# Decode attention with a gated feed-forward: K turned by VectorE in 32x32 blocks instead of by TensorE through PSUM

## The chip, the cores and the metric

One core of one Trainium2 chip. The time is device microseconds of one execution of the whole program; the kernel before takes 231.77 us, the median of three runs (231.77 to 231.87). Engines are named as the profile names them: PE (TensorE), PEld (its weight loads), DVE (VectorE), ACT (ScalarE), POOL (GpSimd), and SP, whose queue issues nearly all DMA transfers.

## The reference, cut to what matters

```
xn = layernorm(x)                                   # x: [2, 1, 512], two sequences, one new token each
q  = (xn @ wq) as 32 heads of 128                   # 8 K/V heads, 4 query heads to each
k, v = the last 4096 positions of k_cache, v_cache  # [2, 8, 4096, 128] of [2, 8, 32768, 128]
p  = softmax(q . k / sqrt(128)) over the 4096 positions
A  = (p . v as [2, 4096]) @ wo
B  = ((gate * (gate > 0)) * up) @ W_down            # gate = xn @ W_gate, up = xn @ W_up, 1792 wide
out = x + A + B                                     # [2, 1, 512], all float32
```

## The kernel before

All data are float32. Everything large is read once: wq, W_gate and W_up, then K and V, then W_down and wo, 94.9 MB together.

**Loads.** `load` (L69) takes a tile from the pool `ring`, which has four slots (`RING = 4`, L17), and issues one transfer on SP's queue (L71). A load waits until the tile that had its slot four loads earlier has been read for the last time; later loads wait behind it on the same queue. The order of the loads through the ring is wq in two halves, W_gate, W_up, then for groups 0 to 3 the K tiles, with the V tiles of the group before in between: k0_0, k0_1, k1_0, v0_0, k1_1, v0_1, k2_0, v1_0, k2_1, v1_1, k3_0, v2_0, k3_1, v2_1, v3_0, v3_1, then W_down and wo in two halves (wo0, wo1; wo1 in five pieces).

**Groups.** A group g is one sequence and four K/V heads (`C = 4`), so there are `NG = 4` groups. A K or V tile (g, a), with a = 0 or 1, holds two heads h: partitions are 64 blocks of 64 consecutive positions for each of the two heads interleaved with them (row p = 2y + h), and each row has 64 positions times 128 values (4.19 MB).

**From K to scores.** `transposes` (L248) turns K on PE: 64 products with the identity for each tile, 128x128 each (L256), four to a PSUM bank, and each bank is copied to the tile kT in SBUF (L245), by ACT and DVE in turn. `scores` (L262) multiplies kT with the query columns qz (L269): 16 products a tile, over the 128 values of a head, 512 positions each, four of them at a time in the four quarters of PE's columns. `kwork` (L375) delays scores by half a tile and places the steps of the last group's `softmax` (L275) between the transposes, step by step, so that PE, DVE and ACT work on different banks at the same time.

**Softmax and values.** `softmax` finds the maximum (L278, L281, L283, L287, L293, L297), takes the exponential on ACT with its row sums (L302), turns the probabilities on PE (L313) and copies them out with a mask (L314). `values` (L326) multiplies them with the V tile (L333, 16 products) and DVE masks the result into `on` (L339). `gather` (L346) sums over rows on PE (L350), `finish` (L355) adds up and scales (L360, L361), and `spread_heads` (L363) puts two finished groups into the layout of the last projection (L366).

**Order.** The pool is under a manual schedule: each engine runs its instructions in the order of the program text (the loops from L391 on), and waits where an operand or a buffer is not ready. For each group g from 1 to 3 and each a: load k(g, a), load v(g-1, a), K work of (g, a) with softmax of g-1 inside it where a = 0, then values of (g-1, a). After the loops come the last softmax, the last values, the products with W_down and wo (L430, L434) and the output.

Of the kernel before, what the change touches and what calls it, by code (L numbers as in the profile page):

```python
# [20 lines left out]
def kernel(  # L21
# [89 lines left out]
    NSLOT = C * S1  # L111
    qz = const.tile([P, NG, NSLOT * 36], F32, name="qz")
    nc.gpsimd.memset(qz, 0.0)
    ones = const.tile([1, 1], F32, name="ones")
# [7 lines left out]
    spread = const.tile([HR, NE, HR, NE], F32, name="spread")  # L122
    nc.gpsimd.memset(spread, 0.0)
    for e in range(NE):
        nc.gpsimd.tensor_copy(spread[:, e, :, e], ident[0:HR, 0:HR])
# [18 lines left out]
    by_h = const.tile([P, NP, HK], F32, name="by_h")  # L144
    nc.vector.tensor_reduce(
        out=by_h, in_=ident.rearrange("p (q a s k) -> p a k q s", q=Q, a=NP, s=S1), op=ALU.add, axis=AX.XY
    )

    half_of = const.tile([P, 2], F32, name="half_of")
    nc.vector.tensor_reduce(  # L150
        out=half_of, in_=ident.rearrange("p (y h) -> p h y", h=2), op=ALU.add, axis=AX.X
    )
    own = const.tile([P, 2, REP], F32, name="own")
    nc.vector.tensor_copy(own, half_of[:, :, None].to_broadcast([P, 2, REP]))

# [18 lines left out]
    xn = const.tile([B, D], F32, name="xn")  # L174
# [29 lines left out]
    for r in range(R):  # L204
        qs = work.tile([P, 512], F32, name=f"qs{r}", tag="qs")
        (nc.vector.tensor_copy if r else nc.scalar.copy)(qs, q_ps[r])
        qt = ps_kt.tile([P, REP, C, 16, B], F32, name=f"qt{r}", tag="kt")
        for i in range(REP):
            nc.tensor.transpose(  # L209
                qt[:, i].rearrange("p c s b -> p (c s b)"), qs[:, i * P:(i + 1) * P], ident  # L210
            )
        for b in range(B):
            dst = qz[:, r * B + b].rearrange("p (a s h k) -> p a s h k", a=NP, s=S1, h=2)
            for h in range(2):
                nc.vector.tensor_copy(  # L215
                    dst[:, :, :, h, 0:REP], qt[:, :, h::2, 0:S1, b].rearrange("p i a s -> p a s i")
                )

# [12 lines left out]
    gr = work.tile([P, FQ], F32, name="gr", tag="gr", bufs=1)  # L231
# [7 lines left out]
    HW = W // S1  # L239
    ss, pts, rls = {}, {}, {}  # L240
    kts, osb = {}, {}
    turn = [0]

    def evacuate(dst, src):
        (nc.vector.tensor_copy if turn[0] % 2 else nc.scalar.copy)(dst, src)  # L245
        turn[0] += 1

    def transposes(g, a, s1, kt_in):  # L248

        kt = ktp.tile([P, 2, HW], F32, name=f"kT{g}_{a}_{s1}", tag="kT")  # L250
        kts[g, a, s1] = kt
        for n in range(2 * Q):
            pk = ps_kt.tile([P, 512], F32, name=f"pk{g}_{a}_{s1}_{n}", tag="kt")
            for u in range(4):
                j = 8 * Q * s1 + 4 * n + u
                nc.tensor.transpose(pk[:, u * P:(u + 1) * P], kt_in[:, j * P:(j + 1) * P], ident)  # L256
            evacuate(
                kt[:, :, n * 256:(n + 1) * 256], pk.rearrange("p (y h) -> p h y", h=2),
            )
            yield  # L260

    def scores(g, a, s1):  # L262
        if (a, s1) == (0, 0):
            ss[g] = ps_s.tile([P, 512], F32, name=f"s{g}", tag="s")
        kt = kts.pop((g, a, s1))
        for h in range(2):
            n = (a * S1 + s1) * 2 + h
            for q in range(Q):
                nc.tensor.matmul(  # L269
                    ss[g][32 * q:32 * q + 32, :], qz[:, g, 32 * n:32 * n + 32],  # L270
                    kt[:, h, q * 512:(q + 1) * 512],
                    start=(a == 0 and s1 == 0 and h == 0), stop=(a == NP - 1 and s1 == S1 - 1 and h == 1),
                )

    def softmax(g):  # L275

        m = work.tile([P, 1], F32, name=f"m{g}", tag="m")
        nc.vector.tensor_reduce(out=m, in_=ss[g], op=ALU.max, axis=AX.X)  # L278
        yield
        mt = ps_1.tile([1, P], F32, name=f"mt{g}", tag="misc")  # L280
        nc.tensor.transpose(mt, m, ident)  # L281
        mx = work.tile([1, NP, HK], F32, name=f"mx{g}", tag="mx")
        nc.vector.tensor_reduce(  # L283
            out=mx, in_=mt.rearrange("p (q a s k) -> p a k q s", q=Q, a=NP, s=S1), op=ALU.max, axis=AX.XY
        )
        mb = work.tile([1, NP, S1, HK], F32, name=f"mb{g}", tag="mb")
        nc.vector.tensor_scalar(  # L287
            mb, mx[:, :, None, :].to_broadcast([1, NP, S1, HK]), -SCALE, None, op0=ALU.mult
        )
        yield  # L290
        nm_ps = ps_1.tile([P, 1], F32, name=f"nm_ps{g}", tag="misc")
        for q in range(Q):
            nc.tensor.matmul(  # L293
                nm_ps[32 * q:32 * q + 32, :], mb.rearrange("p a s k -> p (a s k)"), ones, start=True, stop=True
            )
        nm = work.tile([P, 1], F32, name=f"nm{g}", tag="nm")
        nc.vector.tensor_copy(nm, nm_ps)  # L297

        p = work.tile([P, 512, 2], F32, name=f"p{g}", tag="p", bufs=1)
        l = work.tile([P, 1], F32, name=f"l{g}", tag="l")  # L300
        both = ss[g][:, :, None].to_broadcast([P, 512, 2])
        nc.scalar.activation(p, both, AF.Exp, bias=nm, scale=SCALE, accum_out=l)  # L302
        yield
        yield
        yield

        pts[g] = work.tile([P, 2, Q * NP * S1, 4, HK], F32, name=f"pt{g}", tag="pt")
        pv = p.rearrange("r y h -> r (y h)")
        for jh in range(2):
            pp = ps_kt.tile([P, 4, P], F32, name=f"pp{g}_{jh}", tag="kt")  # L310
            for u in range(4):
                lo = (4 * jh + u) * P
                nc.tensor.transpose(pp[:, u], pv[:, lo:lo + P], ident)  # L313
            nc.vector.tensor_tensor(  # L314
                pts[g][:, jh].rearrange("p n u k -> p u n k"), pp.rearrange("p u (n k) -> p u n k", k=HK),
                own.rearrange("p h i -> p (h i)")[:, None, None, :].to_broadcast([P, 4, Q * NP * S1, HK]), op=ALU.mult,
            )
            yield
        lp = ps_1.tile([HR, 1], F32, name=f"lp{g}", tag="misc")
        nc.tensor.matmul(lp, by_h.rearrange("p a k -> p (a k)"), l, start=True, stop=True)  # L320
        rls[g] = work.tile([HR, 1], F32, name=f"rl{g}", tag="rl")
        nc.vector.reciprocal(rls[g], lp)
# [3 lines left out]
    def values(g, a, v):  # L326
        o = ps_1.tile([P, 512], F32, name=f"o{g}_{a}", tag=f"o{a}")
        for s1 in range(S1):
            for jh in range(2):
                for q in range(Q):  # L330
                    n = (q * NP + a) * S1 + s1
                    lo = (8 * Q * s1 + 8 * q + 4 * jh) * P
                    nc.tensor.matmul(  # L333
                        o[32 * q:32 * q + 32, :],
                        pts[g][:, jh, n].rearrange("p u k -> p (u k)"), v[:, lo:lo + 512],
                        start=(s1 == 0 and jh == 0), stop=(s1 == S1 - 1 and jh == 1),
                    )
# [17 lines left out]
    def finish(g):  # L355
        r, b = divmod(g, B)
        if b == 0:
            osb[r] = const.tile([HR, B, P], F32, name=f"osb{r}")
        od = work.tile([HR, P], F32, name=f"od{g}", tag="od")
        nc.vector.tensor_reduce(out=od, in_=oa[g].rearrange("h u d -> h d u"), op=ALU.add, axis=AX.X)  # L360
        nc.vector.tensor_scalar(osb[r][:, b], od, rls[g], 2.0, op0=ALU.mult, op1=ALU.mult)  # L361

    def spread_heads(r):  # L363
        op = ps_1.tile([P, NJ, B], F32, name=f"op{r}", tag="misc")
        for e in range(NE):
            nc.tensor.matmul(  # L366
                op, spread[:, e].rearrange("h k e -> h (k e)"),
# [5 lines left out]
    pend = []  # L373

    def kwork(g, a, kt_in, others=()):  # L375

        others = list(others)
        for s1 in range(S1):
            for n, _ in enumerate(transposes(g, a, s1, kt_in)):
                if n > 1 and others and next(others[0], "end") == "end":  # L380
                    others.pop(0)
                if (a, s1, n) == (0, 0, 1) and pend:
                    scores(*pend.pop())
            if pend:
                scores(*pend.pop())
            pend.append((g, a, s1))
        for o in others:
            for _ in o:
                pass

    for a in range(NP):  # L391
        kwork(0, a, load_kv(k_cache, "k", 0, a))
    for g in range(1, NG):
        for a in range(NP):
            kt_in = load_kv(k_cache, "k", g, a)
            v_in = load_kv(v_cache, "v", g - 1, a)
            kwork(g, a, kt_in, [softmax(g - 1)] if a == 0 else [])
            if a:
                gather(g - 1, a - 1)
# [6 lines left out]
    scores(*pend.pop())  # L406
    vin = [load_kv(v_cache, "v", g, a) for a in range(NP)]
    dw = load_down()
    for _ in softmax(g):
        pass  # L410
# [43 lines left out]
    yw = work.tile([P, D], F32, name="yw", tag="yw", bufs=1)  # L454
# [38 lines left out]
```

## Time and profile before

| | before |
|---|---|
| time, median of 3 runs (us) | 231.77 |
| profiled execution: time / span of its instructions (us) | 231.71 / 229.9 |
| busy, share of the span: PE / PEld / DVE / ACT | 79% / 42% / 32% / 20% |
| bytes read from HBM, mean rate over the span | 94.90 MB, 413 GB/s |
| mean granted PE clock, share of full speed | 0.925 |

How to read it: the span runs from the first to the last instruction of the profiled execution; its time contains it and 1.8 us around it. A busy share is an average over stages. In lists of groups a row gives line, engine, operation, output<-inputs, shapes and count, then busy time in all and the mean duration of one in ns, then the idle time ahead of them and who ended it. In the chain of waits and in timelines a row begins with start and duration in us. In the view by windows a row has the stretch, then for PE, PEld, DVE, ACT and POOL the busy time and count, then granted PE clock, busy share of the DMA engines, and GB/s. On PE a float32 product shows as two records.

### The profile page before, as it was taken

Reading aid. Unit: us, or ns where it says so; the run is one execution under the profiler, and the core shown is the slowest. Engines: PE = TensorE matmul, PEld = TensorE weight load, DVE = VectorE, ACT = ScalarE, POOL = GpSimd, SP = SyncE. Lnnn points to the kernel's source line nnn. Section 1 sums busy time; section 2 is a strip of 40 time slices with the busy share of each in tenths; the row PEclk is TensorE's granted clock in tenths of the full one; section 3 lists DMA queues with packets and bytes.
Section 4 is the critical chain, followed back from the end, with each engine's and each line's share of the span. In section 5 each row is a group of like instructions: output and inputs, shape, how many; then the busy total and the mean of one; then the engine's idle time right before and its main releaser. Section 6 shows DMA issues by size and latency. Waiting matters only on the chain.

```text
span 229.9 us, 3250 instructions
## 1 busy us (share of the span) xinstructions
PE 182.2 (79%) x1432; PEld 96.0 (42%) x1432; DVE 73.3 (32%) x143; ACT 46.6 (20%) x78; POOL 3.8 (2%) x17
## 2 busy tenths in 40 slices
PE   0483970819999889998899699589999965889493
PEld 0430230219666573661583563248566213124011
DVE  2400021024444561641572441247244144111000
ACT  2000100004444550440351340025134002000001
POOL 6000000000000000000000000000000000000000
PEclk9998598576999999999999999889999996799799
DMA  7999999999999999999999999999999999999980
GB/s 274 456 433 391 464 409 466 399 445 450 422 408 450 436 410 423 448 428 413 439 450 419 416 446 442 410 422 456 425 410 436 445 422 430 428 445 405 420 339 14
DMA packets 3921, 95.10 MB, mean 414 GB/s; under 512 B 442, under 2 KB 450, under 8 KB 836
## 3 DMA queue, kind: packets, MB, share of 16 engines
q1 hardware_dynamic: 3896, 94.90, 96.4%
q8 instruction: 11, 0.18, 0.3%
q14 instruction: 2, 0.02, 0.0%
q10 hardware_dynamic: 12, 0.01, 0.0%
HBM read 94.90 MB, written 0.00 MB: 413 GB/s over the span
## 4 chain that ended last, share of the span: by engine, by line
PE 51%; DMA 41%; DVE 4%; ACT 2%; issue 1%; SPq 1%
DMA k<-in_A_k_cache_dram 25%; PE pk L256 23%; PE s L269 11%; DMA wo<-in_A_wo_dram 10%; PE o L333 9%; DMA wq<-in_A_wq_dram 5%; PE q_ps L198 3%; PE pp L313 2%; ACT p L302 2%; PE oa L350 2%; DVE kT L245 1%; PE op L366 1%; SPq L449 1%; DVE on L339 1%; PE nm_ps L293 0%
## 5 line engine op out<-in xcount | busy, mean ns | idle before, releaser
L256 PE MATMUL pk<-ident,k 128*128 128x128 f32 x512 | 67.3, 286 | 8.4 <-DMA k<-in_A_k_cache_dram 8.4
L256 PEld LDWEIGHTS pk<-ident,k 128*128 128x128 f32 x512 | 57.7, 146 | 24.6 <-issue 21.0
L245 ACT COPY kT<-pk 128x512 f32<-128x512 f32 x64 | 37.5, 586 | 100.1 <-PE pk L256 100.1
L245 DVE COPY kT<-pk 128x512 f32<-128x512 f32 x64 | 44.2, 691 | 37.9 <-PE pk L256 37.8
L333 PE MATMUL o<-v,pt 128*32 128x512 f32 x256 | 34.2, 627 | 0.0
L269 PE MATMUL s<-kT,qz 128*32 128x512 f32 x256 | 32.1, 607 | 0.0
L339 DVE TENSOR_TENSOR on<-o,own_u 128x512 f32<-128x512 f32 x8 | 5.5, 692 | 39.4 <-PE o L333 39.4
L333 PEld LDWEIGHTS o<-v,pt 128*32 128x32 f32 x256 | 8.9, 114 | 20.0 <-issue 19.9
L198 PE MATMUL q_ps<-wq,xnT 128*32 128x512 f32 x64 | 12.3, 940 | 4.3 <-DMA wq<-in_A_wq_dram 4.3
L269 PEld LDWEIGHTS s<-kT,qz 128*32 128x32 f32 x256 | 7.0, 111 | 13.2 <-issue 13.2
L350 PE MATMUL oa<-on,pick 128*16 128x512 f32 x16 | 8.2, 596 | 4.2 <-DVE on L339 4.2
L430 PE MATMUL yw_ps<-wo,oT 128*2 128x512 f32 x56 | 7.9, 703 | 3.9 <-DMA wo<-in_A_wo_dram 3.9
L186 PE MATMUL xt_ps<-rep,xn 2*128 2x32 f32 x16 | 3.7, 402 | 8.7 <-DVE rep L179 8.7
L225 PE MATMUL u_ps<-wu,xnT 128*32 128x448 f32 x32 | 5.2, 816 | 6.6 <-DMA wu<-in_B_W_up_dram 6.6
L198 PEld LDWEIGHTS q_ps<-wq,xnT 128*32 128x32 f32 x64 | 2.9, 163 | 12.9 <-issue 7.6
L313 PE MATMUL pp<-ident,p 128*128 128x128 f32 x32 | 5.5, 306 | 2.4 <-ACT p L302 1.5
L455 ACT COPY yw<-yw_ps 128x512 f32<-128x512 f32 x1 | 0.6, 586 | 33.3 <-PE yw_ps L430 33.3
L186 PEld LDWEIGHTS xt_ps<-rep,xn 2*128 2x128 f32 x16 | 3.6, 319 | 8.7 <-DVE rep L179 8.7
L302 ACT ACTIVATE p<-s,nm 128x1024 f32<-128x1024 f32 x4 | 4.5, 1115 | 13.0 <-DVE nm L297 12.9
L314 DVE TENSOR_TENSOR pt<-pp,own 128x512 f32<-128x512 f32 x8 | 5.5, 692 | 3.8 <-PE pp L313 3.7
L215 DVE COPY qz<-qt 128x16 f32<-128x16 f32 x8 | 0.8, 167 | 17.6 <-PE qt L209 17.6
L225 PEld LDWEIGHTS u_ps<-wu,xnT 128*32 128x32 f32 x32 | 1.3, 160 | 10.5 <-DMA wu<-in_B_W_up_dram 7.4
(72 smaller groups left out, 60.9 us busy)
## 6 DMA issues: line engine op xcount, KB each, us to landing
k<-in_A_k_cache_dram SPq DMA_DIRECT2D x8, 4096.0 KB, 29.1
v<-in_A_v_cache_dram SPq DMA_DIRECT2D x8, 4096.0 KB, 29.0
wq<-in_A_wq_dram SPq DMA_DIRECT2D x2, 4096.0 KB, 16.9
wo<-in_A_wo_dram SPq DMA_DIRECT2D x1, 4096.0 KB, 31.7
wg<-in_B_W_gate_dram SPq DMA_DIRECT2D x1, 3584.0 KB, 29.6
wu<-in_B_W_up_dram SPq DMA_DIRECT2D x1, 3584.0 KB
wd<-in_B_W_down_dram SPq DMA_DIRECT2D x1, 3584.0 KB
wo<-in_A_wo_dram SPq DMA_DIRECT2D x1, 2048.0 KB, 20.7
```

Source lines behind the costliest of these rows:

```text
L186: nc.tensor.matmul(xt_ps[:, v, kc, :], lhsT, rep16.rearrange("r s b -> r (s b)"), start=True, stop=True)
L198: nc.tensor.matmul(q_ps[r][32 * c:32 * c + 32, :], xnT[:, 0, kc, :], wqt[kc // 2][:, kc % 2, n * 512:(n + 1) * 512], start=(kc == 0), stop ...
L225: nc.tensor.matmul(dst[32 * c:32 * c + 32, :], xnT[:, 1, kc, :], wt[:, kc, c * FQ:(c + 1) * FQ], start=(kc == 0), stop=(kc == KC - 1),)
L245: (nc.vector.tensor_copy if turn[0] % 2 else nc.scalar.copy)(dst, src)
L256: nc.tensor.transpose(pk[:, u * P:(u + 1) * P], kt_in[:, j * P:(j + 1) * P], ident)
L269: nc.tensor.matmul(ss[g][32 * q:32 * q + 32, :], qz[:, g, 32 * n:32 * n + 32], kt[:, h, q * 512:(q + 1) * 512], start=(a == 0 and s1 == 0 ...
L302: nc.scalar.activation(p, both, AF.Exp, bias=nm, scale=SCALE, accum_out=l)
L313: nc.tensor.transpose(pp[:, u], pv[:, lo:lo + P], ident)
L333: nc.tensor.matmul(o[32 * q:32 * q + 32, :], pts[g][:, jh, n].rearrange("p u k -> p (u k)"), v[:, lo:lo + 512], start=(s1 == 0 and jh == 0 ...
L339: nc.vector.tensor_tensor(ons[a], o.rearrange("p (u d) -> p u d", u=4), own_u[:, :, None].to_broadcast([P, 4, P]), op=ALU.mult)
L350: nc.tensor.matmul(oa[g].rearrange("h u d -> h (u d)"), pick[:, 8 - 8 * a:24 - 8 * a], ons[a].rearrange("p u d -> p (u d)"), start=(a == 0 ...
L430: nc.tensor.matmul(yw_ps[32 * c:32 * c + B, :], lhsT, w, start=(n < Q), stop=(n >= wide - Q))
```

## The change

K is no longer turned by PE. For each half tile DVE turns 32x32 blocks of [128, 4096] values with four `transpose` instructions of 128x1024, from SBUF to SBUF (new function `keys`). After that, a lane quarter (32 partitions) of kT holds 32 of the 128 values of a head, for the 32 rows of K that lay in that quarter. A score product therefore runs over 32 values (index m) for four sets of positions at once: its weights qz hold the query in block-diagonal form, one block for each lane quarter x, and m = 0 to 3 accumulates in PSUM. There are still 16 products of 512 columns for each tile; their moving operand takes every second element (`h::2`), because the two heads alternate in the turned rows.

The 16 products read the turned tile whole, and the pool for kT has room for one tile (two halves), as before.

The probabilities go into pz, every second element for each head, in two exponentials of 64 partitions; DVE turns pz in 32x32 blocks, and 16 copies of 32 partitions, by ACT and DVE in turn, move the blocks to the lane quarters where V needs them. The softmax of group g now stands in the program text right after the scores of (g, 1), as one piece, ahead of gather and values of group g-1; the step-by-step interleaving is gone. The setup of qz is done by 32 small copies on ACT and DVE, some constants are smaller or share memory, and a factor 2 is taken elsewhere.

```diff
+    JS = J // S1
+    NB = DH // 32
+    qz = const.tile([P, NG, NB, NP, 2, 32], F32, name="qz")
     nc.gpsimd.memset(qz, 0.0)
+    pz = const.tile([P, JS, 32], F32, name="pz")
+    nc.gpsimd.memset(pz, 0.0)
...
+        for m in range(NB):
+            src = qt[32 * m:32 * m + 32, :, :, 0].rearrange("p i (t h) b -> p b t h i", h=2)
+            for x in range(Q):
+                d = qz[32 * x:32 * x + 32, r * B:r * B + B, m]
+                dst = bass.AP(
+                    tensor=d.tensor, offset=d.offset + x * TK,
+                    ap=[d.ap[0], d.ap[1], [64 + REP, NP], [32, 2], [1, REP]],
                 )
+                (nc.vector.tensor_copy if x % 2 else nc.scalar.copy)(dst, src)
...
-    def transposes(g, a, s1, kt_in):
...
-    def scores(g, a, s1):
...
+    CUT = 4
+
+    def keys(g, a, kt_in):
+
+        if a == 0:
             ss[g] = ps_s.tile([P, 512], F32, name=f"s{g}", tag="s")
+        kts = []
+        for s1 in range(S1):
+            kt = ktp.tile([P, JS, NB, 32], F32, name=f"kT{g}_{a}_{s1}", tag="kT")
+            n = JS // CUT
+            for c in range(CUT):
+                lo = (s1 * JS + c * n) * DH
+                nc.vector.transpose(
+                    kt[:, c * n:(c + 1) * n].rearrange("p j m k -> p (j m k)"), kt_in[:, lo:lo + n * DH]
                 )
+            kts.append(kt)
+        for m in range(NB):
+            for h in range(2):
+                for s1 in range(S1):
+                    q = 2 * h + s1
+                    nc.tensor.matmul(
+                        ss[g][32 * q:32 * q + 32, :], qz[:, g, m, a, h], kts[s1][:, :, m, h::2],
+                        start=(a == 0 and m == 0), stop=(a == NP - 1 and m == NB - 1),
+                    )
...
+        pv = pz.rearrange("p j (i h) -> p j i h", h=2)
+        for h in range(2):
+            o = slice(PK * h, PK * h + PK)
+            nc.scalar.activation(
+                pv[o, :, :, h], ss[g][o].rearrange("p (j i) -> p j i", j=JS), AF.Exp, bias=nm[o], scale=SCALE, accum_out=l[o],
             )
+        pT = work.tile([P, JS, Q, NP, REP], F32, name=f"pT{g}", tag="pT", bufs=1)
+        nc.vector.transpose(pT.rearrange("p j x t k -> p (j x t k)"), pz.rearrange("p j s -> p (j s)"))
+        pts[g] = work.tile([P, NP, S1, JS, 2, REP], F32, name=f"pt{g}", tag="pt")
+        n = 0
+        for h in range(2):
+            for s1 in range(S1):
+                q = 32 * (2 * h + s1)
+                for x in range(Q):
+                    (nc.vector.tensor_copy if n % 2 else nc.scalar.copy)(
+                        pts[g][32 * x:32 * x + 32, :, s1, :, h], pT[q:q + 32, :, x].rearrange("p j t k -> p t j k")
+                    )
+                    n += 1
...
     for a in range(NP):
-        kwork(0, a, load_kv(k_cache, "k", 0, a))
+        keys(0, a, load_kv(k_cache, "k", 0, a))
+    softmax(0)
     for g in range(1, NG):
         for a in range(NP):
             kt_in = load_kv(k_cache, "k", g, a)
             v_in = load_kv(v_cache, "v", g - 1, a)
-            kwork(g, a, kt_in, [softmax(g - 1)] if a == 0 else [])
+            keys(g, a, kt_in)
             if a:
+                softmax(g)
                 gather(g - 1, a - 1)
             elif g % B == 1 and g > 1:
                 spread_heads((g - 2) // B)
...
     g = NG - 1
-    scores(*pend.pop())
     vin = [load_kv(v_cache, "v", g, a) for a in range(NP)]
     dw = load_down()
-    for _ in softmax(g):
-        pass
```

More of the change, by code (lines that the diff above doesn't have):

```diff
@@ L109 @@
     make_identity(nc, ident)
-    NSLOT = C * S1
-    qz = const.tile([P, NG, NSLOT * 36], F32, name="qz")
+    JS = J // S1
+    NB = DH // 32
+    qz = const.tile([P, NG, NB, NP, 2, 32], F32, name="qz")
     nc.gpsimd.memset(qz, 0.0)
+    pz = const.tile([P, JS, 32], F32, name="pz")
+    nc.gpsimd.memset(pz, 0.0)
     ones = const.tile([1, 1], F32, name="ones")
@@ L120 @@
     oT = const.tile([P, R, NJ, B], F32, name="oT")
-    spread = const.tile([HR, NE, HR, NE], F32, name="spread")
+    spread = const.tile([HR, HR + 1, NE], F32, name="spread")
     nc.gpsimd.memset(spread, 0.0)
-    for e in range(NE):
-        nc.gpsimd.tensor_copy(spread[:, e, :, e], ident[0:HR, 0:HR])
+    nc.gpsimd.tensor_copy(spread[:, 0:HR, NE - 1], ident[0:HR, 0:HR])
     pick = const.tile([P, 24], F32, name="pick")
@@ L143 @@
     HK = 2 * REP
[L144 to L154, printed above, removed]
+    TK = NP * REP
+    by_h = const.tile([P, NP, 2, REP], F32, name="by_h")
+    for h in range(2):
+        nc.vector.tensor_reduce(
+            out=by_h[:, :, h], in_=ident[:, PK * h:PK * h + PK].rearrange("p (x t k) -> p t k x", t=NP, k=REP),
+            op=ALU.add, axis=AX.X,
+        )
     stats = const.tile([B, 6], F32, name="stats")
@@ L173 @@
     nc.vector.tensor_scalar(xc, x2, mv[:, 0:1], 2.0, op0=ALU.subtract, op1=ALU.mult)
-    xn = const.tile([B, D], F32, name="xn")
+    xn = xc
     nc.vector.tensor_scalar(xn, xc, rs2, None, op0=ALU.mult)
@@ L211 @@
             )
[L212 to L216, printed above, removed]
+        for m in range(NB):
[5 more added lines that the diff above has]
+                    ap=[d.ap[0], d.ap[1], [64 + REP, NP], [32, 2], [1, REP]],
                 )
+                (nc.vector.tensor_copy if x % 2 else nc.scalar.copy)(dst, src)
     g_ps = ps_kt.tile([P, FQ], F32, name="g_ps", tag="kt")
@@ L230 @@
     nc.scalar.copy(gs, g_ps)
-    gr = work.tile([P, FQ], F32, name="gr", tag="gr", bufs=1)
+    gr = gs
     nc.vector.scalar_tensor_tensor(gr, gs, 0.0, gs, op0=ALU.is_gt, op1=ALU.mult)
@@ L235 @@
     nc.vector.transpose(hT, hh.rearrange("p (w k) -> p k w", k=FB))
-    HW = W // S1
     ss, pts, rls = {}, {}, {}
[L241 to L246, printed above, removed]
-    def transposes(g, a, s1, kt_in):
[L250 to L260, printed above, removed]
-    def scores(g, a, s1):
-        if (a, s1) == (0, 0):
-            ss[g] = ps_s.tile([P, 512], F32, name=f"s{g}", tag="s")
[L265 to L272, printed above, removed]
-                )
+    osb = {}
+    CUT = 4
+    def keys(g, a, kt_in):
+        if a == 0:
+            ss[g] = ps_s.tile([P, 512], F32, name=f"s{g}", tag="s")
+        kts = []
[6 more added lines that the diff above has]
+                    kt[:, c * n:(c + 1) * n].rearrange("p j m k -> p (j m k)"), kt_in[:, lo:lo + n * DH]
+                )
+            kts.append(kt)
[7 more added lines that the diff above has]
+                    )
     def softmax(g):
@@ L278, in softmax @@
         nc.vector.tensor_reduce(out=m, in_=ss[g], op=ALU.max, axis=AX.X)
-        yield
         mt = ps_1.tile([1, P], F32, name=f"mt{g}", tag="misc")
         nc.tensor.transpose(mt, m, ident)
-        mx = work.tile([1, NP, HK], F32, name=f"mx{g}", tag="mx")
+        mx = work.tile([1, 2, TK], F32, name=f"mx{g}", tag="mx")
         nc.vector.tensor_reduce(
-            out=mx, in_=mt.rearrange("p (q a s k) -> p a k q s", q=Q, a=NP, s=S1), op=ALU.max, axis=AX.XY
+            out=mx, in_=mt.rearrange("p (h x k) -> p h k x", h=2, k=TK), op=ALU.max, axis=AX.X
@@ L285, in softmax @@
         )
-        mb = work.tile([1, NP, S1, HK], F32, name=f"mb{g}", tag="mb")
+        mb = work.tile([1, 2, S1 * Q, TK], F32, name=f"mb{g}", tag="mb")
         nc.vector.tensor_scalar(
-            mb, mx[:, :, None, :].to_broadcast([1, NP, S1, HK]), -SCALE, None, op0=ALU.mult
+            mb, mx[:, :, None, :].to_broadcast([1, 2, S1 * Q, TK]), -SCALE, None, op0=ALU.mult
         )
-        yield
         nm_ps = ps_1.tile([P, 1], F32, name=f"nm_ps{g}", tag="misc")
[L292 to L295, printed above, removed]
+        nc.tensor.matmul(nm_ps, mb.rearrange("p h x k -> p (h x k)"), ones, start=True, stop=True)
@@ L296, in softmax @@
         nm = work.tile([P, 1], F32, name=f"nm{g}", tag="nm")
         nc.vector.tensor_copy(nm, nm_ps)
-        p = work.tile([P, 512, 2], F32, name=f"p{g}", tag="p", bufs=1)
         l = work.tile([P, 1], F32, name=f"l{g}", tag="l")
[L301 to L316, printed above, removed]
-            )
-            yield
+        pv = pz.rearrange("p j (i h) -> p j i h", h=2)
@@ L319, in softmax @@
+        n = 0
+        for h in range(2):
+            for s1 in range(S1):
[3 more added lines that the diff above has]
+                        pts[g][32 * x:32 * x + 32, :, s1, :, h], pT[q:q + 32, :, x].rearrange("p j t k -> p t j k")
+                    )
+                    n += 1
         lp = ps_1.tile([HR, 1], F32, name=f"lp{g}", tag="misc")
-        nc.tensor.matmul(lp, by_h.rearrange("p a k -> p (a k)"), l, start=True, stop=True)
+        nc.tensor.matmul(lp, by_h.rearrange("p t h k -> p (t h k)"), l, start=True, stop=True)
@@ L330, in values @@
                 for q in range(Q):
-                    n = (q * NP + a) * S1 + s1
-                    lo = (8 * Q * s1 + 8 * q + 4 * jh) * P
+                    j = 16 * jh + 4 * q
+                    lo = (JS * s1 + j) * P
                     nc.tensor.matmul(
                         o[32 * q:32 * q + 32, :],
-                        pts[g][:, jh, n].rearrange("p u k -> p (u k)"), v[:, lo:lo + 512],
+                        pts[g][:, a, s1, j:j + 4].rearrange("p u h k -> p (u h k)"), v[:, lo:lo + 512],
                         start=(s1 == 0 and jh == 0), stop=(s1 == S1 - 1 and jh == 1),
@@ L360, in finish @@
         nc.vector.tensor_reduce(out=od, in_=oa[g].rearrange("h u d -> h d u"), op=ALU.add, axis=AX.X)
-        nc.vector.tensor_scalar(osb[r][:, b], od, rls[g], 2.0, op0=ALU.mult, op1=ALU.mult)
+        nc.vector.tensor_scalar(osb[r][:, b], od, rls[g], None, op0=ALU.mult)
     def spread_heads(r):
@@ L366, in spread_heads @@
             nc.tensor.matmul(
-                op, spread[:, e].rearrange("h k e -> h (k e)"),
+                op, spread.rearrange("h k e -> h (k e)")[:, NE - 1 - e:NE - 1 - e + P],
                 osb[r][:, :, e * NJ:(e + 1) * NJ].rearrange("h b j -> h j b"),
@@ L371, in spread_heads @@
         nc.vector.tensor_copy(oT[:, r], op)
[L373 to L382, printed above, removed]
-                    scores(*pend.pop())
[L384 to L388, printed above, removed]
-                pass
     for a in range(NP):
-        kwork(0, a, load_kv(k_cache, "k", 0, a))
+        keys(0, a, load_kv(k_cache, "k", 0, a))
+    softmax(0)
     for g in range(1, NG):
@@ L405 @@
     g = NG - 1
-    scores(*pend.pop())
     vin = [load_kv(v_cache, "v", g, a) for a in range(NP)]
     dw = load_down()
-    for _ in softmax(g):
-        pass
     y_ps = ps_kt.tile([P, P], F32, name="y_ps", tag="kt")
@@ L453 @@
             project_wide(oT[:, r, j], wots[r][:, j])
-    yw = work.tile([P, D], F32, name="yw", tag="yw", bufs=1)
+    yw = work.tile([P, D], F32, name="yw", tag="on")
     nc.scalar.copy(yw, yw_ps)
```

## Prediction

> **What bounds the kernel now.** The page comes first: it says whether an engine or the transfers set the end.
>
> ```profile
> span 229.9 us, 3250 instructions
> ...
> DMA  7999999999999999999999999999999999999980
> ...
> q1 hardware_dynamic: 3896, 94.90, 96.4%
> ```
>
> The DMA digits are 9 in all slices but the first and the last two, and the packets of SP's queue fill 96.4% of the span of all 16 DMA engines, 221.6 us of 229.9. So the transfers bound the kernel; PE, at 79%, is second. A change of the arithmetic can win almost nothing (the 8 us that are left are start and end, which this change does not touch), but it can lose, if it holds ring slots until the queue runs dry. The second view, the chain of waits, cut to its longest pieces, gives the clock of the transfers.
>
> ```profile
> 0.73 12.24 DMA wq<-in_A_wq_dram
> 13.11 6.03 PE q_ps L198 x32
> 19.16 31.70 DMA k<-in_A_k_cache_dram
> 50.99 9.62 PE pk L256 x64
> 121.52 26.47 DMA k<-in_A_k_cache_dram
> 195.01 5.52 PE o L333 x32
> ```
>
> The first K tile lands at 19.16 + 31.70 = 50.86 us, the tile k3_0, ten loads later, at 147.99: 9.71 us for each tile, 38.9 us for the four tiles (two of K, two of V) of a group. The first row shows a transfer on an empty queue: 12.24 us. After 50.86 us the question is one only: do the engines get through a group in 38.9 us?
>
> **What is removed.** From the list of groups:
>
> ```profile
> L256 PE MATMUL pk<-ident,k 128*128 128x128 f32 x512 | 67.3, 286 | 8.4 <-DMA k<-in_A_k_cache_dram 8.4
> ...
> L245 DVE COPY kT<-pk 128x512 f32<-128x512 f32 x64 | 44.2, 691 | 37.9 <-PE pk L256 37.8
> ```
>
> PE loses 67.3 us, DVE 44.2 us, ACT as many copies. All of it lay under the transfers, so this gives nothing by itself. With it goes the overlap: PE turned one bank while DVE and ACT emptied others.
>
> **Turning a tile on DVE (T).** A tile is 8 instructions of 128x1024. The trace has one instruction of this kind, of another size and with a strided input (14 floats apart), and a plain reduction whose input steps by two floats.
>
> ```profile
> L235 DVE STREAM_TRANSPOSE hT<-hh 128x448 f32<-128x448 f32 x1 | 0.9, 936 | 0.0
> ...
> L150 DVE TENSOR_REDUCE half_of<-ident 128x2 f32<-128x128 f32 x1 | 0.3, 275 | 0.0
> ```
> ```profile
> 4.76 0.28 DVE L134 TENSOR_REDUCE own_u<-ident 128x4 f32<-128x128 f32 x1
> 4.96 0.36 DVE L138 TENSOR_REDUCE fold<-ident 128x32 f32<-128x128 f32 x1
> ```
>
> From 128 elements in 275 ns to 512 in 691 ns is 1.083 ns an element and 136 ns fixed; 1024 elements would take 1.245 us. The next instruction starts 0.08 us before the one ahead ends (4.96 against 4.76 + 0.28), so 8 take 8 x 1.165 = 9.3 us. The other end is the transpose's own row scaled: 936/448 x 1024 = 2.14 us, T = 8 x 2.06 = 16.5 us. I take 9.3, because that row's input is strided and strides show as cost elsewhere: L138, whose input steps by 32 floats, takes 0.36 us for the same 128 elements as L134 in 0.28. Below lies two elements a cycle (a rival). [...]
>
> **The score products (S).** Still 16 a tile with 512 columns, four at a time. From the chain:
>
> ```profile
> 60.62 1.85 PE s L269 x16
> ...
> 88.46 3.43 PE o L333 x32
> ```
>
> 32 records are 2 x 1.85 = 3.7 us, and values of a tile (V) 3.4 us, at full clock. The clock is what changes, as the view by windows shows:
>
> ```profile
> 46.40:51.00 4.60, 0.01 (x1) 0.04 (x1) 1.56 (x2) 0.00 (x0) 0.00 (x0) 0.74 0.93 399
> 51.00:55.40 4.40, 4.40 (x21) 4.40 (x22) 1.38 (x2) 1.17 (x2) 0.00 (x0) 0.50 1.04 447
> ...
> 194.90:198.80 3.90, 3.90 (x24) 0.99 (x24) 0.00 (x0) 0.00 (x0) 0.00 (x0) 0.50 1.00 426
> ```
>
> After 4.6 us without products the granted clock was 0.50 for the next 4.4 us of work. The values that began in such a stretch (195.01) took 5.52 us instead of 3.43: 2.1 us more. During T, PE now has nothing to do for 9.3 us, so every burst behind a T starts at half clock: S = 5.8 us, S and V together 3.7 + 3.4 + 2.1 = 9.2. The moving operand takes every second float; on PE no row shows this. It costs nothing (in L150, which steps so on DVE, nothing is seen) up to double, 7.4 us; I take nothing.
>
> **Where DVE stops.** All of T must be done before S can finish its first four products. T of the next tile writes the same kT buffers, so it waits for S. In group g's first half, DVE's next instruction in program order is moreover the mask `on` of values(g-1, 0), which waits for V; the 8 transposes of (g, 1) are queued behind it. So T, S, V and T come one after another; before, they overlapped.
>
> **The softmax in one piece.** The last softmax of before runs alone and shows it:
>
> ```profile
> 188.23 0.69 DVE L278 TENSOR_REDUCE m<-s 128x1 f32<-128x512 f32 x1 [0.78 <-PE s L269]
> 189.29 0.28 DVE L283 TENSOR_REDUCE mx<-mt 1x16 f32<-1x128 f32 x1 [0.36 <-PE mt L281]
> 189.60 0.17 DVE L287 TENSOR_SCALAR mb<-mx 1x32 f32<-1x32 f32 x1
> 190.21 0.16 DVE L297 COPY nm<-nm_ps 128x1 f32<-128x1 f32 x1 [0.44 <-PE nm_ps L293]
> ```
> ```profile
> 190.40 1.22 ACT p L302 x2
> ```
>
> Maximum to exponential is 190.40 + 1.22 - 188.23 = 3.4 us. Two exponentials of half the length cost 1.22 to 2.44; with 1.6 the stretch is 3.8 us. Then DVE turns pz (1.2) and does 8 of 16 copies of 256 elements (0.2 at two elements a cycle to 0.41 by the slope above; 3.0 in all with the reciprocal, ACT's 8 beside them): 4.4 us with waits. From group 1 on this lies beside PE's gather and values(g-1, 1): 1.0 + 4.5 = 5.5 us. (4.5 lies between 3.4 and 5.5, as the 3.8 us ahead of it are a little shorter than the idle stretch above.) Then DVE and PE finish the group, as at the end of before:
>
> ```profile
> 205.85 0.69 DVE L339 TENSOR_TENSOR on<-o,own_u 128x512 f32<-128x512 f32 x1 [4.61 <-PE o L333]
> 207.67 0.68 DVE L360 TENSOR_REDUCE od<-oa 16x128 f32<-16x512 f32 x1 [1.12 <-PE oa L350]
> 208.38 0.28 DVE L361 TENSOR_SCALAR osb<-od,rl 16x128 f32<-16x128 f32 x1
> ```
>
> From `on` to `osb` that is 2.8 us, and only then does DVE reach T of the next group.
>
> **Costs of nothing.** The 32 copies of qz, the memset of pz and the smaller constants lie before 50.86 us, where PE waits for K (4.6 us idle in the row 46.40:51.00). Were that cover gone, each us would count in full. The sharing of memory (xn, gr, yw) joins tiles whose uses are already in sequence.
>
> **The sum**, for the profiled execution. Group 0, without values: T 9.3, S 5.8, T 9.3, S 5.8, softmax 3.8 + 4.4, together 38.4; from 50.9 to 89.3 us. Groups 1 to 3: T 9.3, S and V 9.2, `on` 0.75, T 9.3, S 5.8, softmax 3.8, gather and V 5.5, finish 2.8, together 46.5, against 38.9 of transfers: 3 x 46.5 = 139.4. Group 3 has also `spread_heads`, 2.0 (below). That is 230.7 us. The queue falls behind at about 99 us: k2_0 needs the slot of k1_0, whose T ends at 89.3 + 9.3 = 98.6, while the transfer ahead of it lands at 50.86 + 5 x 9.71 = 99.4; later issues fall further behind. The tail, by PE's timeline:
>
> ```profile
> 194.40 0.60 PE L416 MATMUL y_ps<-x,ident 2*2 2x128 f32 x8 [0.89 <-DVE y_ps L414]
> ...
> 210.99 1.97 PE L366 MATMUL op<-osb,spread 16*128 16x32 f32 x16
> 216.35 6.90 PE L430 MATMUL yw_ps<-wo,oT 128*2 128x512 f32 x48 [3.39 <-DMA wo<-in_A_wo_dram]
> 223.78 1.04 PE L430 MATMUL yw_ps<-wo,oT 128*2 128x512 f32 x8 [0.52 <-DMA wo<-in_A_wo_dram]
> ```
>
> From y_ps to the end of the spread 18.6 us, the wo products 6.9 + 1.0 = 7.9, from there (224.8) to the end of the span 5.1, of which about 0.6 is waiting for the last piece; with 0.2 for a memset, 31.2 us. wo hides in it: wo0 is issued when values(2, 1) are done, about 228, lands at 240, and wo1 follows 9.7 later at 250, when PE has just got to its products. Span 230.7 + 31.2 = 261.9; the run of 231.71 had 1.8 us around its span, and the median before, 231.77, is as good as that run. Forecast: **264 us**, 14% slower. With T from 8.5 to 10 and the other bounds it is 252 to 276.
>
> **Rivals.**
> - The clock stays up: PE's short products in between, or a luckier phase, keep it at 1.00. Then 2.1 us go from 8 bursts, 1.1 from three values, 2 from the tail: 22 us less, 242. Against: both idle stretches above 4 us that are quoted ended at 0.50.
> - The step of two floats halves PE's reading: S = 7.4 with the half clock hidden in it, 1.6 more on 8 tiles, 13 us: 277. For: no PE row excludes it. [...]
> - T by the transpose's own row: 7.2 more on 8 tiles, 58 us: 321. Against: L138 and L134.
> - Not slower: the transpose runs at two elements a cycle. [...]
>
> ```profile
> L175 DVE TENSOR_SCALAR xn<-xc,rs 2x512 f32<-2x512 f32 x1 | 0.5, 475 | 0.0
> ```
>
>   512 elements in 475 ns are under one cycle each by the slope above. Then T = 8 x (0.53 + 0.08) = 4.9, a group takes 37.7 us, and the transfers bound again: 231.7. It decides from T = 5.5, where the group is 38.9. Against: the transpose's row, 2.1 ns an element.
>
> **How the numbers follow.** Forecast 0.62; clock up 0.14; PE's reading 0.12; slow transpose 0.05; not slower 0.07, of which a gain 0.02 (less than the 8 us outside the transfers). About 0.2% (0.5 us) is what a measurement of this kernel can tell from no change. The range 240 to 282 takes in the forecast and most of the two rivals beside it, some 0.83. Slower 0.93, same 0.05, faster 0.02.
>
> **What would show it.** In the profile after: a group STREAM_TRANSPOSE into kT, x64, mean about 1.24 us; DVE's idle time ahead of `on` and of kT ended by PE; PE clock at 5 to 7 in most slices from 50 us on; DMA digits falling below 9 from about 100 us; SP's queue waiting for DVE's kT; products with wo that no longer wait for a landing. A mean near 2.1 us, score bursts over 7 us, or DMA digits of 9 to the end would each prove a step wrong; the forecast falls if DVE starts a tile's transposes while PE still works on the tile before.

## The result and the profile after

| | before | after |
|---|---|---|
| time, median (us) | 231.77 (231.77 to 231.87) | 264.02 (262.72 to 264.94) |
| ratio to before, 95% interval | | 1.1386 [1.1338, 1.1435] |
| profiled execution: time / span (us) | 231.71 / 229.9 | 262.72 / 260.9 |
| busy us: PE / DVE / ACT | 182.2 / 73.3 / 46.6 | 144.1 / 113.3 / 26.5 |

The change takes 38 us of work from PE and adds 40 to DVE; none of PE, DVE and ACT is busy for more than 55% of the span, and the kernel is 14% slower. The page of after, with the same lines as those shown of before:

```profile
span 260.9 us, 2114 instructions
...
PEclk9997979655659556956686597576858957799999
DMA  8999999999999987999729899992889999669960
...
q1 hardware_dynamic: 3896, 94.90, 86.5%
```

The DMA digits leave 9 in the fifteenth slice, at about 91 to 98 us, and fall below it again and again from there; the transfers no longer bound the kernel. PE's granted clock lies between 5 and 7 in most slices from about 50 us. Who holds the transfers back is told by SP's queue in the view of waits (us in total, times, longest):

```profile
SPq L71 <- DVE kT L253: 96.6, 8, 23.0
SPq L71 <- PE o L318: 60.2, 5, 16.8
```

A ring slot that holds a K tile (the first row counts 8 waits for one) now comes free when DVE has turned the tile. Waiting there cost nothing while older transfers filled the queue (DMA digits of 9 up to 91 us); from about 98 us on it did. The list of groups has the new work:

```profile
L253 DVE STREAM_TRANSPOSE kT<-k 128x1024 f32<-128x1024 f32 x64 | 73.0, 1206 | 10.8 <-PE s L261 6.0 <-DMA k<-in_A_k_cache_dram 4.8
L261 PE MATMUL s<-kT,qz 128*32 128x512 f32 x256 | 60.1, 885 | 72.2 <-DVE kT L253 72.2
```

The transposes take 1206 ns each, 73.0 us together. PE stands idle 72.2 us ahead of the score products, waiting for them, and its program order gives it nothing else to do in that time. (The 60.1 us busy include the first product of each tile, which starts when half the tile is turned: two records that took 1.9 us. PE is then idle for another 2.5 us, until the rest is turned.) The chain of waits, from the start of group 1 to the start of group 2:

```profile
89.35 9.14 DVE kT L253 x8
...
98.53 4.48 PE s L261 x19
...
103.98 3.48 PE o L318 x30
...
108.09 9.13 DVE kT L253 x8
...
117.26 6.24 PE s L261 x30
...
123.52 0.70 DVE m L269
...
127.53 0.21 PE lp L305 x2
...
129.48 5.11 PE o L318 x27
...
137.14 0.27 DVE osb L346
137.42 9.05 DVE kT L253 x8
```

This is the loss in ten lines: T, S with V, mask, T, S, softmax, V, finish, one behind the other, 137.42 - 89.35 = 48.1 us against the 38.9 us that the transfers of a group need.

### The profile page after: what moved, and what is told of

The parts are those of the page before. It is cut to its first block, busy times and chain, and to the rows that moved or that the text cites. A ratio compares the mean times of both kernels' runs of the same rounds, so it can differ in the third digit from the quotient of the medians.

```text
span 260.9 us, 2114 instructions
## 1 busy us (share of the span) xinstructions
PE 144.1 (55%) x864; PEld 40.3 (15%) x864; DVE 113.3 (43%) x178; ACT 26.5 (10%) x70; POOL 3.7 (1%) x11
## 3 DMA queue, kind: packets, MB, share of 16 engines
q1 hardware_dynamic: 3896, 94.90, 86.5%
## 4 chain that ended last, share of the span: by engine, by line
PE 42%; DVE 34%; DMA 17%; ACT 3%; issue 2%; ACTq 0%
DVE kT L253 27%; PE s L261 17%; PE o L318 13%; DMA k<-in_A_k_cache_dram 12%; DMA wq<-in_A_wq_dram 5%; PE oa L335 4%; PE yw_ps L396 4%; ACT pz L289 2%; PE q_ps L195 2%; PE op L351 1%; DVE on L324 1%; DVE m L269 1%; DVE pt L300 1%; DVE od L345 1%; PE nm_ps L281 1%
## 5 line engine op out<-in xcount | busy, mean ns | idle before, releaser
L261 PE MATMUL s<-kT,qz 128*32 128x512 f32 x256 | 60.1, 885 | 72.2 <-DVE kT L253 72.2
L253 DVE STREAM_TRANSPOSE kT<-k 128x1024 f32<-128x1024 f32 x64 | 73.0, 1206 | 10.8 <-PE s L261 6.0
L318 PE MATMUL o<-v,pt 128*32 128x512 f32 x256 | 40.9, 699 | 0.0
L261 PEld LDWEIGHTS s<-kT,qz 128*32 128x32 f32 x256 | 10.9, 147 | 118.7 <-DVE kT L253 80.4
L324 DVE TENSOR_TENSOR on<-o,own_u 128x512 f32<-128x512 f32 x8 | 5.5, 692 | 38.4 <-PE o L318 38.4
L289 ACT ACTIVATE pz<-s,nm 64x512 f32<-64x512 f32 x8 | 5.6, 703 | 120.2 <-DVE nm L283 120.1
L300 ACT COPY pt<-pT 32x256 f32<-32x256 f32 x32 | 12.9, 402 | 5.6 <-DVE pT L293 5.2
L300 DVE COPY pt<-pT 32x256 f32<-32x256 f32 x32 | 9.1, 285 | 0.5
L293 DVE STREAM_TRANSPOSE pT<-pz 128x1024 f32<-128x1024 f32 x4 | 5.0, 1245 | 8.2 <-ACT pz L289 8.2
L183 PE MATMUL xt_ps<-rep,xc 2*128 2x32 f32 x16 | 3.7, 402 | 8.4 <-DVE rep L176 8.4
L225 PE MATMUL g_ps<-wg,xnT 128*32 128x448 f32 x32 | 4.8, 759 | 0.0
```

Of the source, the lines that this page charges most:

```text
L183: nc.tensor.matmul(xt_ps[:, v, kc, :], lhsT, rep16.rearrange("r s b -> r (s b)"), start=True, stop=True)
L253: nc.vector.transpose(kt[:, c * n:(c + 1) * n].rearrange("p j m k -> p (j m k)"), kt_in[:, lo:lo + n * DH])
L261: nc.tensor.matmul(ss[g][32 * q:32 * q + 32, :], qz[:, g, m, a, h], kts[s1][:, :, m, h::2], start=(a == 0 and m == 0), stop=(a == NP - 1 a ...
L289: nc.scalar.activation(pv[o, :, :, h], ss[g][o].rearrange("p (j i) -> p j i", j=JS), AF.Exp, bias=nm[o], scale=SCALE, accum_out=l[o],)
L300: (nc.vector.tensor_copy if n % 2 else nc.scalar.copy)(pts[g][32 * x:32 * x + 32, :, s1, :, h], pT[q:q + 32, :, x].rearrange("p j t k -> p ...
L318: nc.tensor.matmul(o[32 * q:32 * q + 32, :], pts[g][:, a, s1, j:j + 4].rearrange("p u h k -> p (u h k)"), v[:, lo:lo + 512], start=(s1 == ...
```

## The experiments

In these runs before took 231.63 and 231.67 us (medians). Two theories stood against each other at first. Series: each group is one chain, and every piece of it that is hidden gives its own length back. Clock: the half clock after each pause of PE (0.50 in before's row 51.00:55.40, 0.59 in after's S at 117.20) is what makes the group longer than its transfers. Beside them stood PE's reading of every second float, and a slowing of the transfers by VectorE's traffic.

**T twice.**

```diff
-                nc.vector.transpose(
-                    kt[:, c * n:(c + 1) * n].rearrange("p j m k -> p (j m k)"), kt_in[:, lo:lo + n * DH]
-                )
+                for _ in range(2):
+                    nc.vector.transpose(
+                        kt[:, c * n:(c + 1) * n].rearrange("p j m k -> p (j m k)"), kt_in[:, lo:lo + n * DH]
+                    )
```

> Every transpose of K is done twice, into the same place; nothing else differs. Series theory (T, S, V, T, S, softmax, V and finish follow one another, so T lies wholly on the path): T goes from 9.1 to about 18.3 us and the time grows by 8 x 9.1 = 73 us, from 264 to 337. Rival, that VectorE has room (43% busy) and something else sets the pace: clearly less than 73 us, under 300. Rival, that VectorE's traffic slows the transfers: packets longer than the 1213 ns of 32 KB seen before.

Measured: 345.2 us, 81.2 more than after. The timeline of DVE for the first two tiles:

```profile
50.64 19.37 DVE L254 STREAM_TRANSPOSE kT<-k 128x1024 f32<-128x1024 f32 x16 [4.82 <-DMA k<-in_A_k_cache_dram]
75.89 19.37 DVE L254 STREAM_TRANSPOSE kT<-k 128x1024 f32<-128x1024 f32 x16 [5.88 <-PE s L262]
```

T went from 9.14 to 19.37 us, not 18.3: in the trace the second of a pair, which reads and writes the same places as the first, starts 1.24 us after it, when its 1.20 us are over; the first of the next pair starts 1.17 us after that, before the one ahead has ended. 8 x 10.2 = 82 us were added to DVE and 81 came out at the end, so T lies wholly on the path, although DVE is busy for less than half of after's span. The size expected, 73, was too small for the overlap that was lost; the theory stands. The second row also shows DVE waiting 5.88 us for S: that is the kT buffer, in group 0, where there are no values.

**PE kept at work.** Nine products a tile on constant data; their result is not used.

```diff
             kts.append(kt)
+        fill = ps_kt.tile([P, 448], F32, name=f"fill{g}_{a}", tag="kt")
+        for _ in range(FILL):
+            nc.tensor.matmul(fill[0:32, :], qz[:, 0, 0, 0, 0], hT[:, 0:FB, :].rearrange("p k w -> p (k w)"), start=True, stop=True)
         for m in range(NB):
```

> Nine products on constant data (448 columns each, into a spare PSUM bank, result unused) are put ahead of each tile's score products, so that TensorE is at work while VectorE turns the tile. Clock theory (the half clock after each T is what makes S 5.3 to 6.2 us): granted clock near 1.0 in the K stage, S about 3.7 us, 15 to 23 us less in all, 241 to 249. Rival, that reading every second float limits S: S stays above 5 us with the clock up, and the time stays within 5 us of 264. Series theory: whatever the clock, the time stays over 238, since T, S, V and softmax still follow one another.

Measured: 253.66 us, ratio to before 1.0947 [1.093, 1.0963]: 10.4 us less than after, short of the 15 to 23 expected. One row of the view by windows and one of PE's timeline, for the second tile of group 1:

```profile
115.00:118.80 3.80, 3.71 (x30) 0.93 (x30) 0.02 (x1) 0.00 (x0) 0.00 (x0) 1.00 0.98 414
```
```profile
115.01 3.71 PE L265 MATMUL s<-kT,qz 128*32 128x512 f32 x30 [3.19 <-DVE kT L254]
```

At a clock of 1.00 the products take 3.71 us, as the 3.7 of before with contiguous data; after had 6.24 for the same tile, at a clock of 0.59. (Two of the 32 records, those of the first product, ran ahead of this row.) So the step of two floats cost PE nothing here, and the clock alone made S long. The gain fell short because the products fill only the time of T: the first S of a group still met a clock of 0.66, and the values behind the softmax 0.72:

```profile
96.20:101.20 5.00, 4.92 (x32) 1.40 (x36) 0.03 (x1) 0.00 (x0) 0.00 (x0) 0.66 0.87 334
...
123.00:129.00 6.00, 6.00 (x34) 1.39 (x29) 3.46 (x10) 3.22 (x8) 0.00 (x0) 0.72 0.68 295
```

The series theory's floor of 238 held with room to spare: a group still took 44.7 us.

**One mask moved.** Only the mask of values(g-1, 0) is put behind the transposes of (g, 1) on DVE; `between` runs behind the transposes of a tile.

```diff
-            keys(g, a, kt_in)
+            keys(g, a, kt_in, (lambda: mask(g - 1, 0, o)) if a else None)
...
-            values(g - 1, a, v_in)
+            o = values(g - 1, a, v_in)
+        mask(g - 1, 1, o)
         gather(g - 1, NP - 1)
```

> One instruction a group is moved: the mask of values(g-1, 0) stands on VectorE behind the transposes of (g, 1) instead of ahead of them; the products keep their order. Series theory in its detail (the 8 transposes were queued behind that mask, which waits for V): V 3.5 and mask 0.6 leave the path, 4.1 us for each of three groups, about 12 us less, 252. Rival, that the kT buffer alone holds T back until S is done, and the mask costs only its own 0.6: 2 us less, 262.

Measured: 252.23 us, ratio 1.0879 [1.0821, 1.0937], 11.8 less than after; 12 were expected, and the rival's 2 are refuted. DVE's timeline, first of after, then of this run:

```profile
89.35 9.13 DVE L253 STREAM_TRANSPOSE kT<-k 128x1024 f32<-128x1024 f32 x8
107.48 0.69 DVE L324 TENSOR_TENSOR on<-o,own_u 128x512 f32<-128x512 f32 x1 [9.00 <-PE o L318]
108.09 9.12 DVE L253 STREAM_TRANSPOSE kT<-k 128x1024 f32<-128x1024 f32 x8
```

```profile
89.84 9.13 DVE L253 STREAM_TRANSPOSE kT<-k 128x1024 f32<-128x1024 f32 x8
104.50 9.13 DVE L253 STREAM_TRANSPOSE kT<-k 128x1024 f32<-128x1024 f32 x8 [5.53 <-PE s L263]
113.55 0.65 DVE L329 TENSOR_TENSOR on<-o,own_u 128x512 f32<-128x512 f32 x1
```

Between the two T lie 5.53 us of waiting for S (the buffer), where after had 9.00 of waiting for S and V and then the mask. One small instruction in the wrong place of an engine's order cost 12 us.

**Values first.** Order alone: PE does the values of group g-1 while DVE turns the tile; mask behind T, gather behind S, finish behind the softmax.

```diff
-            keys(g, a, kt_in)
+            os = []
+            keys(g, a, kt_in, lambda: os.append(values(g - 1, a, v_in)))
+            mask(g - 1, a, os[0])
+            gather(g - 1, a)
             if a:
                 softmax(g)
-                gather(g - 1, a - 1)
+                finish(g - 1)
             elif g % B == 1 and g > 1:
                 spread_heads((g - 2) // B)
-            values(g - 1, a, v_in)
-        gather(g - 1, NP - 1)
-        finish(g - 1)
```

> Order alone: the value products of group g-1 stand ahead of the score products of the tile, so TensorE does them while VectorE turns the tile; their mask stands behind the transposes of that tile, gather behind the scores, finish behind the softmax. Same instructions, same buffers. Series theory: a group is T 9.1, S 5.8, T 9.1, S 5.8, softmax 4.3 and 3.9, finish 1.0 = 39.0 us against 48.0, about the 38.9 of the transfers; 27 us less, about 236 (234 to 242). Clock theory alone: no more than a few us, over 255. Rival, that VectorE's traffic slows the transfers: over 255 as well, with packets longer than 1213 ns.

Measured: 238.51 us, ratio 1.0286 [1.0262, 1.031]: 25.5 us less than after, by order alone, where the clock theory allowed a few. The groups take 39.3, 37.6 and 38.4 us. The DMA digits of its page:

```profile
DMA  7999999999999989499999999999999999999950
```

One gap is left, near 95 us, where k2_0 waits for the first T of group 1 as in after. What remains above before is the last softmax, which starts 8 us later than before's (196.38 against 188.23), with PE's tail behind it:

```profile
196.38 0.69 DVE m L271
```

A second buffer for kT, which would take away the 3.4 to 5.0 us that T(g, 1) still waits for S in groups 1 and 2, wasn't tried.

**Values first, and PE kept at work.** The order just shown, and `fill(n)` makes n of the products of the second experiment.

```diff
         if between:
             between()
+        fill(5 if between else 9)
         for m in range(NB):
...
+        fill(5)
         nm = work.tile([P, 1], F32, name=f"nm{g}", tag="nm")
```

> The order with the value products first, and with it products on constant data (five behind the value products of a tile and five in each softmax, nine for a tile without values) that keep TensorE at work. If the series of steps and the half clock together are the whole loss, S falls from about 6 to 3.7 us and the last values from 6.5 to 3.5: some 3 us a group and 3 in the tail, so the transfers bound again: 231.5 to 234. If VectorE's traffic or another cost of the new instructions is left over, it stays over 235.

Measured: 234.43 us, ratio 1.0103 [1.0078, 1.0128]; a little over what was expected. Two stretches of its view by windows, the last softmax and the values behind it, and PE's timeline there:

```profile
194.00:203.50 9.50, 5.80 (x26) 1.69 (x24) 6.53 (x18) 4.79 (x12) 0.00 (x0) 0.94 0.97 419
203.50:206.90 3.40, 3.40 (x20) 0.79 (x20) 0.00 (x0) 0.00 (x0) 0.00 (x0) 0.50 0.96 414
```
```profile
196.00 3.94 PE L246 MATMUL fill<-hT,qz 128*32 128x448 f32 x10
...
202.96 0.60 PE L394 MATMUL y_ps<-x,ident 2*2 2x128 f32 x8 [2.99 <-DVE y_ps L392]
203.50 6.47 PE L327 MATMUL o<-v,pt 128*32 128x512 f32 x32
```

The five products ended 3 us before the last values could start, and these met the half clock all the same: 6.47 us instead of the 3.5 hoped for. And where V waits for its transfer (twice, at 142 and 181 us), the extra products stand between V and S and delay S; the second time they are on the chain of waits:

```profile
186.66 3.36 PE fill L246 x9
```

The gap behind the first T of group 1 is there as well (k2_0 is issued at 99.54 us). So 4 us were gained, not 5 to 7: work done to hold the clock up helped only where it stood in nobody's way.

**The softmax between the transposes.** The order with the values first, no extra products; softmax(g-1) is a generator again, a step behind each transpose of (g, 0), finish(g-2) at its end.

```diff
+                if others and next(others[0], "end") == "end":
+                    others.pop(0)
...
-            keys(g, a, kt_in, lambda: os.append(values(g - 1, a, v_in)))
+            keys(g, a, kt_in, lambda: os.append(values(g - 1, a, v_in)), [] if a else [softmax(g - 1)])
...
-            if a:
-                softmax(g)
-                finish(g - 1)
```

> The order with the value products first, and with it the softmax of group g-1 put step by step between the 8 transposes of (g, 0), and finish at their end; no extra products. Series theory: VectorE's waits in the softmax (about 2.7 us a group) are filled with transposes, 39.3 to 36.5 us for a group, below the 38.9 of the transfers; the last softmax starts up to 8 us earlier and the tail with it: 231.5 to 234. Clock theory: without extra products the half clock stays and the time stays near 238.

Measured: 231.99 us, ratio 1.0021 [1.0008, 1.0035]: the whole loss of 32 us but 0.3 is gone, at a mean granted clock of 0.804 (before had 0.925). Three views of it: the page; DVE's timeline at the start of a group; and the last long piece of its chain.

```profile
PEclk9999979765575695699785797985796598599998
DMA  7999999999999999999999999999999999999970
...
q1 hardware_dynamic: 3896, 94.90, 96.1%
```
```profile
115.56 0.69 DVE L279 TENSOR_REDUCE m<-s 128x1 f32<-128x512 f32 x1 [4.79 <-PE s L271]
116.17 1.23 DVE L254 STREAM_TRANSPOSE kT<-k 128x1024 f32<-128x1024 f32 x1
117.33 0.24 DVE L284 TENSOR_REDUCE mx<-mt 1x16 f32<-1x128 f32 x1
117.60 0.22 DVE L288 TENSOR_SCALAR mb<-mx 1x128 f32<-1x128 f32 x1
117.74 1.23 DVE L254 STREAM_TRANSPOSE kT<-k 128x1024 f32<-128x1024 f32 x1
```
```profile
205.86 20.70 DMA wo<-in_A_wo_dram
```

The DMA digits are 9 as before, and the chain ends in the transfer of wo as before. As the first T of group 1 now runs between the steps of the softmax, k2_0 is issued at 96.06 us instead of 98.89 in the version with the values first, and the gap in the digits is gone. Many slices still show a clock of 5 to 7, as in after: a slow PE cost nothing here, where it waits for transfers anyway. So the clock theory, as the whole cause of the loss, is refuted; the half clock was a surcharge on whatever lay on the path, at least 10.4 us in the order of after. No version beat before: the packets fill 96.1% of its 231.1 us.

The same numbers settle the rival that VectorE's traffic slows the transfers: the packets took 96.1% of 231.1 = 222.1 us in all, with all of DVE's new work beside them, against 221.6 before. The median packet of 32 KB took 1213 ns in this run, in after and with T done twice, and 1214 in before. (After, with 86.5% of 260.9 = 225.7, is 4 us above: 137 of its packets took over 1300 ns, against 26 in before, nearly all of them the first ones behind a load that was issued to an empty queue, and they account for 3.6 of the 4 us.)

## Why the prediction was right, point by point

The forecast was 264 us, the result 264.02. So close a hit is in part luck: the groups were forecast 2.6 us too short and the tail 3.6 too long, and the four runs lie between 262.72 and 264.94.

- **T**: 9.3 forecast, 9.14 measured, 1206 ns an instruction. The slope from contiguous rows was right, and the transpose's own row, taken as it stood, would have been wrong by a factor of 1.8. That its strided input made that row long, as the prediction argued, is not shown: no run changes the stride alone. Both rivals on T fell, the one of 4.9 us and the one of 16.5. No run shows a VectorE rate of two elements a cycle, on which the 4.9 and the lower value for a copy of p (0.2) rest: the 1024 elements of a transpose took 1206 ns, the 256 of a copy 285 ns on DVE.
- **S, and S with V**: 5.8 and 9.2 forecast; 5.3 to 6.2, and 107.45 - 98.53 = 8.9, measured. The half clock behind a T was there (0.59 in the row 117.20 below).
- **PE's reading**: taken as free; shown free (3.71 us at a clock of 1.00, with PE kept at work, against the 3.7 of before).
- **Series**: shown by doubling T (81 us of 82) and by taking T's waits away one by one (12, then 25.5, then all but 0.3 us).
- **Softmax**: maximum to exponential 3.8 forecast, 127.49 - 123.52 = 4.0 measured; in group 0 a table load of 1.28 on ACT came on top, which the forecast missed. Turning and copying p 4.4 forecast, 3.8 measured.
- **Gather and values behind the softmax**: 5.5 forecast, 134.59 - 127.53 = 7.1 measured. This is the term of a group that was mis-sized: V was put between full and half clock, and most of it met the half clock. The view by windows of after:

```profile
117.20:123.50 6.30, 6.20 (x30) 1.26 (x30) 0.01 (x1) 0.00 (x0) 0.00 (x0) 0.59 1.00 432
123.50:127.50 4.00, 0.62 (x3) 0.37 (x3) 1.34 (x4) 1.57 (x4) 0.00 (x0) 0.78 1.14 492
127.50:134.60 7.10, 6.99 (x36) 1.67 (x36) 3.69 (x10) 3.22 (x8) 0.00 (x0) 0.64 0.19 81
```

  The row behind the softmax has a clock of 0.64, and gather is slowed with V (0.88 and 0.79 us a record, 0.41 and 0.39 before). The same row shows a DMA share of 0.19: the queue had run dry.
- **The groups**: 46.5 forecast; 48.1 and 47.8 measured, and 48.1 for group 3, where 48.5 were forecast with the spread. The end of the last group came at 233.3 instead of 230.7.
- **The tail**: 31.2 forecast, 260.9 - 233.3 = 27.6 measured. Its first values ran at full clock (3.61 us; the row of before from which the term came had 5.52 at half clock), and the products with wo, which waited for nothing, took 6.2 instead of 7.9.
- **The queue**: k2_0 was forecast to be issued at about 99, at the landing of the transfer ahead of it; it was issued at 98.51, when the DMA digits had just begun to fall.

The rival of the clock was priced at 22 us. Keeping PE at work in T gave 10.4; what the full clock would give where those products did not reach, behind the softmax and in the first S of a group, was not measured alone. The prediction held two idle stretches above 4 us against this rival; its lines show one, 46.40:51.00; in the stretch ahead of 194.90 PE did short products.

## What to carry to other kernels

Compare the chain of one round, not the busy times, with what the bound resource needs for that round: here 48 us against 39 decided, while none of PE, DVE and ACT was busy for more than 55%. When work moves to another engine, look at what stands in that engine's order behind a wait, and who waits behind it; the order of the program text was worth all but 0.3 of the 32 us here, and the new instructions cost almost nothing once they were put beside the waits. A pause of PE made the next burst longer here (6.24 us of S behind a T, 3.71 with PE kept at work), but that counted only where the burst was on the path: the last version lost 0.3 us at a mean clock of 0.804.

## What the runs showed of the hardware that was not expected

- Transposes of 128x1024 that write different places follow each other at 1.14 us (9.14 for 8); when each second one reads and writes the same places as the one ahead, at 1.21 (19.37 for 16).
- A pause of PE of about 3 us behind ten records of work (3.94 us) was followed by a clock of 0.50 for 3.4 us, behind the last softmax of the version with values first and extra products; the forecast had expected 3.8 us to bring only part of it.
- PE's mean clock fell from 0.925 to 0.804 between two kernels whose times differ by 0.2%.
- The first packets behind an idle queue were slow: of after's 137 packets over 1300 ns (median 1213), nearly all follow a load issued to an empty queue.
